# New due times and places for a few instructions in a fused attention and ELU-MLP kernel

## The chip, the cores and the metric

The kernel runs on one core of a Trainium2 chip. The metric is the device time of one execution in microseconds (us). The engines are TensorE (PE, matrix products; PEld its weight loads), VectorE (DVE), ScalarE (ACT), GpSimd (POOL) and SyncE (SP), whose queue issues nearly all DMAs. Each engine works through its own instructions in program order, and an instruction whose data isn't there holds up all behind it.

## The reference

```python
def _attn_ref(q, k, v, cap):            # 4 batches, 12 heads, 448 tokens, 64 wide
    scale = 1.0 / np.sqrt(q.shape[-1])
    scores = scale * np.matmul(q, k.transpose(0, 1, 3, 2))
    scores = cap * np.tanh(scores / cap)
    scores = scores - np.max(scores, axis=-1, keepdims=True)
    attn = np.exp(scores)
    attn = attn / (np.sum(attn, axis=-1, keepdims=True) + 1e-09)
    return np.matmul(attn, v).astype(np.float32)

def _moe_ref(x, w_in, w_out):           # 1792 tokens, 768 -> 2048 -> 768
    h = x @ w_in
    g = np.where(h > 0.0, h, np.exp(np.minimum(h, 0.0)) - 1.0)
    return (g @ w_out).astype(np.float32)
```

The heads of the attention's result, side by side, are the `x` of the second function. The inputs of the second function's weights are 64-bit numbers; the kernel makes 32-bit numbers of them on the chip.

## The kernel before

**Two parts.** The first, some 160 us, is the attention: 48 heads as 24 pairs, in 12 rounds of two pairs. The second is the MLP with its 2048 hidden features as 16 tiles, taken two at a time in 8 layers (r = 0 to 7). Its tokens lie in four blocks of 384, 384, 512 and 512; the first two are half 0 (h = 0), the other two half 1 (h = 1).

**Products.** 32-bit operands are held as a high part and a rest (`high`, `low`), and each product is three matmuls: high by high, rest by high, high by rest (L473, L474, L475). In the later layers, from layer 1 for half 1 and from layer 3 for half 0, the first product of the MLP is done by Strassen's scheme as seven products, numbered 1 to 7 (`block`; `m` in the trace). Some need *forms*: sums of token blocks, which are made once, written to memory (`send`, L351), and read in each layer (`fetch`, L361; `t<-form` in the trace) into a ring of three buffers and two more. A product has three parts in its contraction, so a fetch brings one third of what it needs. A number above 10 in the order means the product of half 0 (13 is product 3 of half 0), a triple such as (1, 1, 0) is the second product of the MLP for two output tiles, of the layer one back, block 1, tiles 0 and 1 (`pair`).

**Weights.** Each of 32 tiles is loaded by one DMA of 768 KB (`load`, L146) into one buffer, and made in steps (`steps`): two on ScalarE (L158, L161), three on VectorE (L169, L172, L185), one addition on GpSimd (L188), a high part and a rest. The step L185 is the last that reads the loaded data, so the next load waits for it.

**What sets the order in attention.** Every piece of work is entered as an event with a time written by hand (`AT`, `END`, `TANH`, `EXP`, in units of one of a round's seven score tiles), and the events, sorted by these times, are the program. The times set the order only. The parts that the change touches: `epsilon` (L1283 to L1288: VectorE, ScalarE, VectorE on one number in each row, which is added to the sums of exponentials), `take` (a numerator copied out of PSUM, L1063), `normalise` (L1092), `weights.run` (weight steps, two in each round that has some; in rounds 2, 5 and 9 it is one, which is L185 with GpSimd's L188), and at the end of attention `weights.run` twice, two steps on ScalarE and three that VectorE does. There `invert` (L1077) turns the sums of the round before the last into reciprocals; SP writes them to memory (L1079), reads them back over all rows (`spread`, L1087), and VectorE multiplies (`normalise`).

**What sets the order in the MLP.** `Plan.run` is a list scheduler. TensorE's order is fixed in the table `ORDERS`. All else is a step with an engine, an assumed duration, a due time, what it needs and gives, and which buffers it takes and frees; for each engine the step with the earliest due among those able to start is put next. Due times come from `DUES` (weights, per layer), `SMALL` (the forms of half 0, made in layers 1 to 3), `EARLY` and `REST` (what follows a product), and `LEAD` (fetches). Assumed times are not in the program: they only decide the order.

Of the kernel before, what the change touches and what calls it, by code (L numbers as in the profile page):

```python
# [53 lines left out]
    "add": ((2.55, 3.2), (6.05, 6.7)),  # L54
    "sums": 9.3, "take": (7.35, 7.95), "take_sums": 10.1,
    "invert": 15.3, "spread": (18.0, 18.01), "normalise": (21.4, 24.85),
    "prep": ((1.5, 1.85), (5.05, 5.4)), "load": (0.3, 5.5), "load_v": (0.2, 0.9),
    "weights": (4.8, 4.9), "wload": -0.5, "split": (-0.25, 1.3), "split_from": 5,
}
# [3 lines left out]

END = {"scored": -2.9, "unit0": 0.3, "weights": (0.5, 0.52)}

# [5 lines left out]
FROM = (3, 1)  # L71
LEAD = -5.1
DUES = (
    (-31.1, -11.1, -10.0, 1.1, 18.5),
    (-22.5, -19.0, -25.9, 2.0, 17.4),
    (-28.5, -23.8, -11.7, 6.1, 13.3),
    (-20.2, -13.3, -5.1, 7.4, 19.4),
)
# [14 lines left out]
    (  # L93
        1, 6, 2, (1, 3, 0), 7, (1, 3, 2), 11, 4, (1, 3, 4), 3, 5, (0, 2, 0), (0, 2, 2), 17, (0, 2, 4), 16,
        (0, 3, 0), (0, 3, 2), 14, 12, 13, 15, (0, 3, 4),
    ),
# [4 lines left out]
    (  # L101
# [3 lines left out]
    ),  # L105
)
SMALL = (-90.7, 23.7, 5.4)
EARLY, REST = (-3.8, -4.5, 4.5, -3.0, 9.6), (-1.1, 4.1, -5.8, -8.0, 2.7)
TAKES = {6: 2, 7: 3, 5: 1, 3: 4}
# [815 lines left out]
class Attention:  # L925
# [168 lines left out]
    def run(self, weights, moe, raw, rawv, scored):  # L1094
# [9 lines left out]
        end = NG * rounds  # L1104
# [5 lines left out]
        for n in range(rounds):  # L1110
# [7 lines left out]
            for i in range(2):  # L1118
# [9 lines left out]
                if p < NPAIR - NORMAL:  # L1128
                    at(min(g + AT["normalise"][i], end + 1.03), self.normalise, p)
                at(g + AT["load"][i], self.load, p + 4)  # L1130
# [8 lines left out]
            for k in range(2):  # L1139
                if k < WROUNDS.get(n, 0):  # L1140
                    at(g + AT["weights"][k], weights.run, 1)
                c = n - AT["split_from"]
                if 0 <= c < NC:
                    at(g + AT["split"][k], *((self.x.high, c, 0) if k == 0 else (self.x.low, c, 0)))
        for time, k in zip(END["weights"], (2, 3)):
            at(end + time, weights.run, k, True)
        for c in range(NC):
            at(end - 2 * NG + 1.5 * c + 1.0, self.x.park, c)
        at(1.5, epsilon, self.nc, self.con)
        at(end + END["scored"], scored)  # L1150
# [280 lines left out]
```

## Time and profile before

| | us |
|---|---|
| runs shown: median (lowest, highest) of 3 | 614.73 (613.46, 617.03) |
| profiled execution, its own time | 613.61 |
| its span, first to last instruction | 611.8 |
| TensorE busy | 597.8 (98%) |
| VectorE busy | 508.5 (83%) |
| ScalarE busy | 368.2 (60%) |
| GpSimd busy | 62.5 (10%) |
| TensorE's waits for fetched forms | 3.5, in two pieces |

The granted clock of TensorE was 0.997 of full over the span, so that no part of it is slowed. Times of the trace are counted from the span's start; the profiled execution's own time holds the span and 1.8 us around it. Where a row ends in square brackets, the engine was idle for so long before it, and what is named ended this.

### The profile page before, as it was taken

How to read it: one execution, taken by the hardware profiler on the slowest of the kernel's cores; microseconds unless marked ns; L12 is line 12 of the kernel's file. 1: busy time of each engine (PE TensorE's matmuls, PEld its weight loads, DVE VectorE, ACT ScalarE, POOL GpSimd, SP SyncE). 2: the span in 40 equal slices, each digit the busy share in tenths (PEclk: the TensorE clock that was granted, in tenths of full speed). 3: DMA queues.
4: the chain of work that ended last, by engine and by line, in shares of the span. 5: the costliest groups of instructions: out<-in, count | busy, mean ns of one | idle time of the engine just before them, and what ended most of it. 6: DMA issues, size and time to landing. Idle time of an engine off the chain costs nothing.

```text
span 611.8 us, 9149 instructions
## 1 busy us (share of the span) xinstructions
PE 597.8 (98%) x3302; PEld 465.4 (76%) x3302; DVE 508.5 (83%) x737; ACT 368.2 (60%) x550; POOL 62.5 (10%) x40
## 2 busy tenths in 40 slices
PE   8999999999999999999999999999999999989996
PEld 4444444444698889988988789898999889889985
DVE  4799999999879986998889888798786978887473
ACT  6999999999876774563564535546263444615130
POOL 0010010010101112111111211111112021111000
PEclk9999999999999999999999999999999999999998
DMA  6445645556421788878866788786678688756924
GB/s 219 147 126 182 219 126 180 176 179 230 150 73 51 293 277 298 304 243 301 295 234 256 284 292 286 276 278 255 241 248 270 250 284 279 243 181 224 307 112 187
DMA packets 61511, 138.49 MB, mean 226 GB/s; under 512 B 12562, under 2 KB 35090, under 8 KB 61458
## 3 DMA queue, kind: packets, MB, share of 16 engines
q1 hardware_dynamic: 61170, 137.30, 65.0%
q8 instruction: 28, 0.46, 0.3%
q10 hardware_dynamic: 288, 0.52, 0.3%
q14 instruction: 25, 0.20, 0.1%
HBM read 117.57 MB, written 20.14 MB: 225 GB/s over the span
## 4 chain that ended last, share of the span: by engine, by line
PE 89%; DMA 5%; DVE 3%; ACT 1%; SPq 1%; issue 1%; DVEq 0%
PE o L474 12%; PE o L475 12%; PE o L473 12%; PE m L473 8%; PE m L474 8%; PE m L475 8%; PE pv L1012 7%; PE s L968 6%; PE h L473 3%; PE h L474 3%; PE h L475 3%; PE sum L1056 3%; DMA t<-form 2%; DMA raw<-in_qk_dram 2%; PE pv L1025 1%; PE s L985 1%
## 5 line engine op out<-in xcount | busy, mean ns | idle before, releaser
L474 PE MATMUL o<-gl,wh 128*128 128x384 f32 (+1 forms) x380 | 137.7, 362 | 0.0
L473 PE MATMUL o<-gh,wh 128*128 128x384 f32 (+1 forms) x380 | 137.7, 362 | 0.0
L475 PE MATMUL o<-gh,wl 128*128 128x384 f32 (+1 forms) x380 | 137.7, 362 | 0.0
L544 DVE TENSOR_TENSOR x<-o,x 128x768 f32<-128x768 f32 (+1 forms) x83 | 89.5, 1085 | 26.5 <-PE o L475 26.4
L188 POOL TENSOR_TENSOR wv<-wv,wq 128x768 int32<-128x768 int32 x24 | 45.9, 1914 | 370.5 <-DVE wv L185 353.1
L1002 ACT ACTIVATE p<-s 128x896 f32<-128x896 f32 x84 | 72.4, 924 | 9.2 <-PE s L985 7.6
L473 PEld LDWEIGHTS o<-gh,wh 128*128 128x128 f32 x380 | 71.3, 188 | 8.1
L474 PEld LDWEIGHTS o<-gl,wh 128*128 128x128 f32 x380 | 71.3, 188 | 7.9
L475 PEld LDWEIGHTS o<-gh,wl 128*128 128x128 f32 x380 | 71.3, 188 | 7.6
L1006 ACT ACTIVATE p<-p 128x896 f32<-128x896 f32 x84 | 74.8, 955 | 0.0
L1012 PE MATMUL pv<-p,vf 128*64 128x448 f32 x276 | 57.2, 548 | 0.0
L158 ACT ACTIVATE wv<-pre 128x768 f32<-128x768 f32 x22 | 19.8, 899 | 47.3 <-DMA pre<-in_w_dram 47.3
L1012 PEld LDWEIGHTS pv<-p,vf 128*64 128x64 f32 x276 | 17.7, 136 | 37.7 <-issue 24.7
L517 ACT ACTIVATE gh<-e 128x384 fp32r<-128x384 f32 (+1 forms) x64 | 35.6, 570 | 16.5 <-DVE e L507 14.7
L521 DVE TENSOR_TENSOR gl<-e,gh 128x384 fp32r<-128x384 f32 (+1 forms) x64 | 40.7, 653 | 4.0 <-ACT gh L517 3.7
L195 ACT ACTIVATE wh<-wv 128x768 fp32r<-128x768 f32 x22 | 18.5, 841 | 42.4 <-POOL wv L188 42.1
L473 PE MATMUL m<-t,forms 128*128 128x512 f32 (+1 forms) x108 | 40.0, 371 | 1.0 <-DMA t<-form 1.0
L474 PE MATMUL m<-t,forms 128*128 128x512 f32 (+1 forms) x108 | 40.1, 371 | 0.0
L475 PE MATMUL m<-t,forms 128*128 128x512 f32 (+1 forms) x108 | 40.0, 370 | 0.0
L502 ACT ACTIVATE e<-c 128x512 f32<-128x512 f32 (+1 forms) x24 | 14.0, 584 | 42.1 <-DVE c L569 42.0
L503 ACT ACTIVATE e<-e 128x384 f32<-128x384 f32 (+1 forms) x64 | 37.1, 579 | 2.0
L569 DVE TENSOR_TENSOR u<-u,m 128x512 f32<-128x512 f32 (+1 forms) x48 | 29.2, 627 | 5.9 <-PE m L475 5.7
(148 smaller groups left out, 1174.3 us busy)
## 6 DMA issues: line engine op xcount, KB each, us to landing
t<-form SPq DMA_DIRECT2D x81, 512.0 KB, 5.4
pre<-in_w_dram SPq DMA_DIRECT2D x32, 768.0 KB, 5.8
t<-form SPq DMA_DIRECT2D x63, 384.0 KB, 5.6
raw<-in_qk_dram SPq DMA_DIRECT2D x22, 448.0 KB, 4.9
form<-t SPq DMA_DIRECT2D x12, 512.0 KB, 3.1
vf<-in_v_dram SPq DMA_DIRECT2D x23, 256.0 KB, 5.4
rb<-rec SPq DMA_DIRECT2D x48, 112.0 KB, 2.9
form<-stage SPq DMA_DIRECT2D x12, 384.0 KB, 4.0
```

Source lines behind the costliest of these rows:

```text
L188: nc.gpsimd.tensor_tensor(out=vi, in0=vi, in1=q, op=ALU.add)
L473: mm(acc, wh[:, m, :], ph, start=first, stop=False)
L474: mm(acc, wh[:, m, :], pl, start=False, stop=False)
L475: mm(acc, wl[:, m, :], ph, start=False, stop=last)
L503: self.nc.scalar.activation(out=e, in_=e, func=AF.Exp, scale=-1.0)
L517: self.nc.scalar.activation(out=self.g[k][0], in_=self.e[k], func=AF.Copy)
L521: self.nc.vector.tensor_tensor(out=gl, in0=self.e.pop(k), in1=gh.bitcast(F32), op=ALU.subtract)
L544: self.nc.vector.tensor_tensor(out=o, in0=self.o.pop((r, t, e)), in1=o, op=ALU.add)
L968: yield lambda a=a, b=b, i=i: self.nc.tensor.matmul(s, a[o, k], b[o, :S], start=i == 0, stop=i == 2)
L1002: self.nc.scalar.activation(out=pt, in_=self.s.pop((n, g)), func=AF.Tanh, scale=self.con.tanh_scale)
L1006: self.nc.scalar.activation(out=pt, in_=pt, func=AF.Exp, scale=self.con.exp_scale)
L1012: self.nc.tensor.matmul(out[o, :S], w[j], x[j], **flags)
```

## The change

It changes numbers in the tables and one line of the rule for rounds with a single weight step.

```diff
-    "sums": 9.3, "take": (7.35, 7.95), "take_sums": 10.1,
+    "sums": 9.3, "take": (6.72, 7.95), "take_sums": 10.1,
...
-    "weights": (4.8, 4.9), "wload": -0.5, "split": (-0.25, 1.3), "split_from": 5,
+    "weights": (4.8, 4.9), "added": 3.05, "wload": -0.5, "split": (-0.25, 1.3), "split_from": 5,
...
-END = {"scored": -2.9, "unit0": 0.3, "weights": (0.5, 0.52)}
+END = {"scored": -2.9, "unit0": 0.3, "weights": (-0.25, -0.24)}
...
-LEAD = -5.1
+LEAD = -4.4
 DUES = (
-    (-31.1, -11.1, -10.0, 1.1, 18.5),
+    (-27.0, -11.1, -20.8, 1.1, 18.5),
...
-        11, (1, 0, 0), 16, (1, 0, 2), 17, (1, 0, 4), 14, (1, 1, 0), 12, 13, (1, 1, 2), 15, (1, 1, 4), 1, 6,
+        11, (1, 0, 0), 16, (1, 0, 2), 17, (1, 0, 4), 13, 14, (1, 1, 0), 12, (1, 1, 2), 15, (1, 1, 4), 1, 6,
...
-SMALL = (-90.7, 23.7, 5.4)
-EARLY, REST = (-3.8, -4.5, 4.5, -3.0, 9.6), (-1.1, 4.1, -5.8, -8.0, 2.7)
+SMALL = (-78.4, 28.7, 5.4)
+EARLY, REST = (-3.8, -4.5, 4.5, -3.0, 12.8), (3.1, 2.6, -15.1, -8.0, 0.8)
...
-                    at(min(g + AT["normalise"][i], end + 1.03), self.normalise, p)
+                    at(min(g + AT["normalise"][i], end + 0.9), self.normalise, p)
...
-                    at(g + AT["weights"][k], weights.run, 1)
+                    alone = WROUNDS[n] == 1
+                    at(g + (AT["added"] if alone else AT["weights"][k]), weights.run, 1)
...
-        at(1.5, epsilon, self.nc, self.con)
+        at(4.6, epsilon, self.nc, self.con)
```

The other three rows of `DUES` change in the same way, and in layer 3 (the fourth table of `ORDERS`) products 11 and 12 each move ahead of one neighbour. From L1130 on every line of the changed file has a number higher by one.

**Attention.** Epsilon's step on ScalarE stood between the exponentials of score tiles 1 and 2 of the first round; it now stands behind that of tile 4. Its two steps on VectorE stood on both sides of L960 and L963 (the parts of a later query and key); they now stand behind the second addition of probabilities (L1046) of the first pair. In rounds 2, 5 and 9 L185, and GpSimd's L188 with it, stood ahead of L960 and L963; it now stands ahead of the copy of the sums (L1068) and of the second L1046 before them. The new times of `take` and `normalise` change no engine's order in rounds 0 to 10.

At the end of attention VectorE's order before was this (`den` the sums that are inverted, `num` a numerator, `wv` the weight tile in its making, `e` and `h` the first values of the MLP):

```order
L1077 RECIPROCAL den10_1801<-den10_1801 64x28
L1063 COPY num22_1867<-pv11_0_1789 128x448
L1092 TENSOR_TENSOR x_123<-num18_1593,rb18_1812 128x448
L169 TENSOR_SCALAR wv3_1872<-wv3_1872 128x768
L172 TENSOR_SCALAR wv3_1872<-wv3_1872 128x768
L185 SCALAR_TENSOR_TENSOR wv3_1872<-pre_73,wv3_1872 128x768
L1063 COPY num23_1880<-pv11_1_1835 128x448
L507 SCALAR_TENSOR_TENSOR e0_0_1908<-e0_0_1908,h0_1848 128x384
L1068 TENSOR_SCALAR sums11_1921<-sum11_1882,eps_88 128x448
```

and it is now:

```order
L1063 COPY num22_1843<-pv11_0_1789 128x448
L169 TENSOR_SCALAR wv3_1845<-wv3_1845 128x768
L172 TENSOR_SCALAR wv3_1845<-wv3_1845 128x768
L185 SCALAR_TENSOR_TENSOR wv3_1845<-pre_73,wv3_1845 128x768
L1077 RECIPROCAL den10_1801<-den10_1801 64x28
L1092 TENSOR_TENSOR x_123<-num18_1584,rb18_1812 128x448
L1063 COPY num23_1880<-pv11_1_1835 128x448
L507 SCALAR_TENSOR_TENSOR e0_0_1908<-e0_0_1908,h0_1858 128x384
L1068 TENSOR_SCALAR sums11_1921<-sum11_1882,eps_88 128x448
```

The inversion and the normalisation behind it now stand behind the copy of the numerator and behind all three weight steps. ScalarE's and SP's orders there are the same as before.

**The MLP, layers 2 and 3, SP's queue.** Rows with `t1_2_1_0<-form1_1_0` are the fetch of half 1, layer 2, form 1, first third; rows with `form0_...<-stage...` are sends of the smaller forms of half 0; `pre<-in_w_dram` is a weight load. Before:

```order
L351 DMA form0_2_2_3273<-stage2_2_3251 128x768
L146 DMA pre_73<-in_w_dram 128x1536
L361 DMA t1_2_1_0_3308<-form1_1_0_2279 128x1024
L361 DMA t1_2_1_1_3328<-form1_1_1_2326 128x1024
L351 DMA form0_4_2_3351<-stage4_2_3316 128x768
L361 DMA t1_2_1_2_3361<-form1_1_2_2379 128x1024
L361 DMA t1_3_2_0_3404<-form1_2_0_2473 128x1024
L146 DMA pre_73<-in_w_dram 128x1536
L361 DMA t1_3_2_1_3447<-form1_2_1_2500 128x1024
L361 DMA t1_3_2_2_3454<-form1_2_2_2545 128x1024
```

and now:

```order
L146 DMA pre_73<-in_w_dram 128x1536
L361 DMA t1_2_1_0_3296<-form1_1_0_2279 128x1024
L351 DMA form0_1_2_3312<-stage1_2_3286 128x768
L361 DMA t1_2_1_1_3334<-form1_1_1_2326 128x1024
L351 DMA form0_3_2_3345<-stage3_2_3310 128x768
L361 DMA t1_2_1_2_3356<-form1_1_2_2379 128x1024
L351 DMA form0_2_2_3380<-stage2_2_3354 128x768
L361 DMA t1_3_2_0_3393<-form1_2_0_2490 128x1024
L361 DMA t1_3_2_1_3415<-form1_2_1_2500 128x1024
L146 DMA pre_73<-in_w_dram 128x1536
L361 DMA t1_3_2_2_3444<-form1_2_2_2519 128x1024
L351 DMA form0_4_2_3467<-stage4_2_3441 128x768
```

Two sends now stand between the three fetches of form 1 where one stood, two more follow among the fetches of layer 3, and a weight load is ahead of the first fetch in both. Elsewhere six loads of weights change places with one neighbouring fetch each.

**The last layer, TensorE.** `m0_7` are the products of half 0 in layer 7, `t0_7_4_2` is the last third of form 4; the pair `o` stands ahead and behind. Before, product 4 came right behind the pair:

```order
L475 MATMUL o6_0_4_5560<-gh13_0_5444,wl27_5159 128x384
L473 MATMUL m4_0_7_5577<-t0_7_4_0_5539,wh29_5377 128x384
L474 MATMUL m4_0_7_5577<-t0_7_4_0_5539,wh29_5377 128x384
L475 MATMUL m4_0_7_5577<-t0_7_4_0_5539,wl29_5378 128x384
L473 MATMUL m4_0_7_5577<-t0_7_4_1_5543,wh29_5377 128x384
L474 MATMUL m4_0_7_5577<-t0_7_4_1_5543,wh29_5377 128x384
L475 MATMUL m4_0_7_5577<-t0_7_4_1_5543,wl29_5378 128x384
L473 MATMUL m4_0_7_5577<-t0_7_4_2_5553,wh29_5377 128x384
L474 MATMUL m4_0_7_5577<-t0_7_4_2_5553,wh29_5377 128x384
L475 MATMUL m4_0_7_5577<-t0_7_4_2_5553,wl29_5378 128x384
L473 MATMUL o6_1_0_5594<-gh12_1_5485,wh26_5056 128x384
```

and now product 3, on `forms` of the weights and resident tokens `x`, comes between (its last three matmuls are shown):

```order
L474 MATMUL m3_0_7_5580<-xl1_5_1829,forms_1895 128x384
L475 MATMUL m3_0_7_5580<-xh1_5_1828,forms_1895 128x384
L473 MATMUL m4_0_7_5594<-t0_7_4_0_5538,wh29_5377 128x384
L474 MATMUL m4_0_7_5594<-t0_7_4_0_5538,wh29_5377 128x384
L475 MATMUL m4_0_7_5594<-t0_7_4_0_5538,wl29_5378 128x384
L473 MATMUL m4_0_7_5594<-t0_7_4_1_5543,wh29_5377 128x384
L474 MATMUL m4_0_7_5594<-t0_7_4_1_5543,wh29_5377 128x384
L475 MATMUL m4_0_7_5594<-t0_7_4_1_5543,wl29_5378 128x384
L473 MATMUL m4_0_7_5594<-t0_7_4_2_5555,wh29_5377 128x384
L474 MATMUL m4_0_7_5594<-t0_7_4_2_5555,wh29_5377 128x384
L475 MATMUL m4_0_7_5594<-t0_7_4_2_5555,wl29_5378 128x384
L473 MATMUL o6_1_0_5609<-gh12_1_5486,wh26_5056 128x384
```

Nine matmuls of product 3 have moved from behind product 2 to ahead of product 4. SP's order of fetches in the last layer is the same.

## Rows read from the trace of the kernel before

**Rows 1.** The page, busy us of each engine, share of the span and instructions

```profile
PE 597.8 (98%) x3302; PEld 465.4 (76%) x3302; DVE 508.5 (83%) x737; ACT 368.2 (60%) x550; POOL 62.5 (10%) x40
```

**Rows 2.** Waits of TensorE: who waited for whom; us in all, times, longest

```profile
PE m L473 <- DMA t<-form: 3.5, 2, 2.5
...
PE sum L1056 <- DVE num L1063: 1.2, 2, 0.9
...
PE h L473 <- DVE e L507: 0.4, 1, 0.4
```

**Rows 3.** Timeline of ScalarE, first round: start, us, engine, line, operation [idle before]

```profile
12.21 0.20 ACT L1287 ACTIVATE eps<-eps 128x1 f32<-128x1 f32 x1 [0.50 <-DVE eps L1284]
12.32 1.77 ACT L1006 ACTIVATE p<-p 128x896 f32<-128x896 f32 x2
```

**Rows 4.** Timeline of TensorE, first round

```profile
18.21 0.47 PE L968 MATMUL s<-qkh 64*128 64x448 f32 x2 [0.71 <-ACT p L1002]
```

**Rows 5.** Timeline of VectorE, round 9, and the subtraction before it

```profile
118.40 1.03 DVE L963 TENSOR_TENSOR qkl<-raw,qkh 128x832 fp32r<-128x832 f32 x1
...
130.15 2.54 DVE L963 TENSOR_TENSOR qkl<-raw,qkh 128x832 fp32r<-128x832 f32 x1
```

**Rows 6.** Timeline of GpSimd, round 9

```profile
129.75 2.05 POOL L188 TENSOR_TENSOR wv<-wv,wq 128x768 int32<-128x768 int32 x1 [48.27 <-DVE wv L185]
```

**Rows 7.** Timeline of VectorE, end of attention

```profile
156.94 0.32 DVE L1077 RECIPROCAL den<-den 64x28 f32<-64x28 f32 x1 [0.25 <-DMA den<-sums]
157.18 0.55 DVE L1063 COPY num<-pv 128x448 f32<-128x448 f32 x1
...
158.87 0.55 DVE L169 TENSOR_SCALAR wv<-wv 128x768 f32<-128x768 f32 x1
...
160.93 0.62 DVE L1063 COPY num<-pv 128x448 f32<-128x448 f32 x1
...
167.20 0.31 DVE L1077 RECIPROCAL den<-den 64x28 f32<-64x28 f32 x1
...
177.34 0.62 DVE L1092 TENSOR_TENSOR x<-num,rb 128x448 f32<-128x448 f32 x1 [0.97 <-DMA rb<-rec]
...
178.96 1.89 DVE L285 TENSOR_TENSOR xl<-x,xh 128x512 fp32r<-128x512 f32 x3
```

**Rows 8.** Timeline of the SP queue, end of attention

```profile
159.80 1.09 SPq L1087 DMA_DIRECT2D rb<-rec  x2
```

**Rows 9.** Instructions of L146 near 161: duration min/median/max, starts; issue to landing

```profile
L146 SPq DMA_DIRECT2D pre<-in_w_dram x1: 433/433/433, 161.1 to 161.1; - x1
...
DMA to landing us min/median/max: 4.8/4.8/4.8
```

**Rows 10.** Instructions of L1071 near 163, the same view

```profile
L1071 SPq DMA_DIRECT2D den<-sums x4: 474/595/597, 162.6 to 164.4; - x4
...
DMA to landing us min/median/max: 2.2/2.6/3.4
```

**Rows 11.** Timeline of TensorE, second part, start

```profile
179.85 0.39 PE L473 MATMUL h<-xh,wh 128*128 128x512 f32 x1
```

**Rows 12.** The fetch (L361) issued at 304.8: us to landing

```profile
DMA to landing us min/median/max: 6.4/6.4/6.4
```

**Rows 13.** Timeline of TensorE, layer 2

```profile
311.88 0.39 PE L473 MATMUL m<-t,forms 128*128 128x512 f32 x1
```

**Rows 14.** Chain that ended last, layer 3: start, us, what

```profile
338.62 7.12 DMA t<-form
```

**Rows 15.** Timeline of TensorE, last layer

```profile
539.72 0.33 PE L473 MATMUL m<-t,forms 128*128 128x384 f32 x1
...
541.28 0.34 PE L473 MATMUL o<-gh,wh 128*128 128x384 f32 x1
...
550.81 0.44 PE L473 MATMUL m<-t,wh 128*128 128x384 f32 x1 [2.53 <-DMA t<-form]
```

**Rows 16.** Chain that ended last, last layer

```profile
544.08 6.69 DMA t<-form
```

More of the change, by code (lines that the diff above doesn't have):

```diff
@@ L71 @@
 FROM = (3, 1)
-LEAD = -5.1
+LEAD = -4.4
 DUES = (
-    (-31.1, -11.1, -10.0, 1.1, 18.5),
-    (-22.5, -19.0, -25.9, 2.0, 17.4),
-    (-28.5, -23.8, -11.7, 6.1, 13.3),
-    (-20.2, -13.3, -5.1, 7.4, 19.4),
+    (-27.0, -11.1, -20.8, 1.1, 18.5),
+    (-20.4, -19.0, -25.9, -8.4, 17.4),
+    (-26.8, -23.1, -11.7, 9.5, 13.3),
+    (-21.9, -13.3, -6.3, 7.4, 16.1),
 )
@@ L93 @@
     (
-        1, 6, 2, (1, 3, 0), 7, (1, 3, 2), 11, 4, (1, 3, 4), 3, 5, (0, 2, 0), (0, 2, 2), 17, (0, 2, 4), 16,
-        (0, 3, 0), (0, 3, 2), 14, 12, 13, 15, (0, 3, 4),
+        1, 6, 2, (1, 3, 0), 7, 11, (1, 3, 2), 4, (1, 3, 4), 3, 5, (0, 2, 0), (0, 2, 2), 17, (0, 2, 4), 16,
+        (0, 3, 0), 12, 14, (0, 3, 2), 13, 15, (0, 3, 4),
     ),
```

## The prediction

> **What bounds the kernel now.** I read the busy times first: TensorE is busy 597.8 of 611.8 us [rows 1], so the end is set by TensorE nearly everywhere, and a change that neither adds nor removes products can move the time only by what TensorE waits. The other engines' shares say little. The waits of TensorE came second: for forms fetched from memory 3.5 us in two pieces, for the copies of the attention numerators 1.2 us in two pieces [rows 2], and single waits below 1 us. The gap that starts the span and the tail behind TensorE's last product are not touched by the change. So I read, thirdly, the instructions around each wait and around each place where an instruction changes its place, on the engine that is waited for: is the late instruction late because of data, or because of its place in the queue?
>
> **The change part by part.**
>
> *Epsilon, at the start.* In the first round ScalarE waits 0.50 us until VectorE has made the first step of epsilon, which stands behind a cast that waits for its data; the pair of exponentials behind it starts at 12.32 [rows 3]. Without epsilon there it starts when ScalarE is free, 12.21 − 0.50 = 11.71, which is 0.61 earlier. Everything ScalarE does next is back to back, and TensorE waits for it once, 0.71 us before 18.21 [rows 4]. So 0.61 of these 0.71 go. Epsilon now stands behind a later exponential, when VectorE's step is long made, and costs ScalarE its own 0.20 [rows 3] at a point where TensorE no longer waits for it. Bounds: −0.71, the whole wait, and 0, if VectorE, which has the same instructions to do in each round, becomes late in ScalarE's place. I take −0.6, since a whole chain starts earlier by it.
>
> *GpSimd's step in rounds 2, 5 and 9.* The step of VectorE that releases GpSimd (L185) moves ahead by some instructions. A subtraction on VectorE (L963) takes 1.03 us alone and 2.54 us where it starts beside GpSimd's addition [rows 5], which runs from 129.75 for 2.05 us [rows 6]. So the collision costs 1.5 us of VectorE, and a later TensorE wait for VectorE's copies (1.2 us in two pieces [rows 2]) stands some microseconds behind two of the three places. After the change GpSimd's addition starts beside the second addition of probabilities (L1046), which reads two operands from on-chip memory as L963 does, and the copies that TensorE waits for stand behind both. So I take the 1.5 us to move from L963 to L1046: VectorE's sum up to the copies stays, and the term is 0. Bounds: −1.2, if L1046 runs free beside GpSimd and both waits go, and +0.9, if the third place gets a wait as long as the longer of the two [rows 2].
> The Trainium skill ("SBUF — State Buffer", section "Who interferes with whom") says that a VectorE instruction with two SBUF inputs and a GpSimd instruction that reads SBUF exclude each other, the first to start blocking the other. The trace agrees for L963 (2.54 against 1.03). By this rule the term is 0; were only L963 open to it, the term would be −1.2.
>
> *End of attention.* This is the part against the change. VectorE inverts the sums of the next-to-last round at 156.94, having waited 0.25 for them, then does a copy, a normalisation and the weight step of three instructions from 158.87 up to 160.93 [rows 7]. The new order puts the copy and these three ahead of the inversion. VectorE is free at 156.94 − 0.25 = 156.69; the copy takes 0.55 and the three 160.93 − 158.87 = 2.06, so the inversion starts at 159.3, 2.35 later. What hangs on it on SP goes in a fixed order: the reciprocals are spread at 159.80 [rows 8], then the load of the next weights at 161.1 [rows 9], then the four issues that collect the last sums, 162.6 to 164.4 [rows 10]. All of it moves by 2.35, except that the four were held only by the sums before: the load ends its issue at 161.1 + 0.43 + 2.35 = 163.9, so they start at about 163.9, 1.3 later. They then land at 164.4 + 1.3 + 2.2 = 167.9 by their own shortest latency [rows 10], or behind the weights, which land 4.8 us after 163.4 [rows 9], at 168.2, plus about 0.65 as before (164.4 + 2.2 = 166.6, against 161.1 + 4.8 = 165.9 for the weights): 168.9. The last inversion was at 167.20 [rows 7], so it is 0.7 to 1.7 late; I take 1.5, nearer to the second, which is what the trace shows of this pair of transfers. The chain goes on through memory without slack: the last normalisation, at 177.34, had waited 0.97 for it, and the subtractions behind it run to 178.96 and on [rows 7], three of them 1.89 us long. They feed TensorE's product at 179.85 [rows 11], whose operand, the first of the three, is done at about 178.96 + 1.89 / 3 = 179.6, some 0.2 earlier. So TensorE loses 1.5 − 0.2 = 1.3. Bounds: −0.4 (TensorE's one wait of 0.4 for the step of VectorE that now comes earlier goes [rows 2], and the collected sums are in time) to +1.9 (the whole shift, less the margins). The weight step that comes earlier earns nothing, since the weights it makes are used far later.
>
> *Layers 1 and 2 of the second part.* Fetches and sends move among each other on SP, for the smaller forms are due 12 us later. The place with least slack: a third fetch is issued at 304.8 and lands 6.4 later [rows 12], at 311.2, for a product at 311.88 [rows 13]: 0.6 to spare. Its issue stands behind a send that VectorE releases, before and after alike; one more 384 KB send now lies in its way on the channels. I take +0.2; bounds 0 (the margin holds) and +0.9.
>
> *Layer 3.* The fetch issued at 338.62 lands 7.12 later and stops TensorE for 1.0 us [rows 14]. SP's order around it, with a weight load ahead of it, is unchanged. I take 0, bounds −0.3 and +0.5.
>
> *Last layer.* TensorE waits 2.53 us before 550.81 [rows 15] for a fetch issued at 544.08 that takes 6.69 [rows 16]. That fetch is issued when the product ahead has given back a buffer, which stays as it is. The new order puts another product, nine matmuls on resident operands, ahead of the product that waits. Nine such take 541.28 − 539.72 = 1.56 us [rows 15]. The other two fetches of that product were in time already. So the wait shrinks by 1.56, and 1.0 to 1.1 of it stays: −1.55. Bounds: −2.53 (the fetch, having more time, is hidden fully) and −1.1, if it lands 0.43 later, by as much as the fetch of layer 3 took longer (7.12 [rows 14]).
>
> *Sum*: −0.6 + 0 + 1.3 + 0.2 + 0 − 1.55 = −0.65. The profiled execution took 613.61 (span 611.8), so its like would take 612.96. The median of the three other runs is 614.73; on it the same sum gives 614.1. I take the middle, 613.5, since one of the three lies far above the others.
>
> **The rivals.**
>
> *The end of attention costs nothing* (faster). For it: the four issues have 2.2 us at the least to land [rows 10], so that with little traffic they would be in time. Against it: the weights' load is in front of them, and the last normalisation waited 0.97 [rows 7], so nothing absorbs a shift. It gives −0.4 in place of +1.3: 613.5 − 1.7 = 611.8, and with the wait of layer 3 gone also, 610.8.
>
> *SP's queue stalls in layer 2* (slower than before). The sends wait for VectorE, and everything behind them on SP waits with them; more of them now stand ahead of fetches. From an issue later than 304.8 + 0.6 = 305.4 the product at 311.88 [rows 13] waits. If VectorE comes to such a send 3 us late, about three of its weight steps (each up to 0.96), TensorE waits 2.4, so the sum is −0.65 − 0.2 + 2.4 = +1.55: 615.7. For it: the 0.6 us are the smallest slack there. Against it: the instruction that releases the send stands where it stood.
>
> *The last layer doesn't gain* (the change doesn't do what it says). If the fetch is issued later by as much as the product moves, the wait stays, and the sum is +0.9: 615.05. Against it: the buffer is given back by a product that comes before both.
>
> **How the numbers follow.** Chances: my forecast 0.5, its own range 612.5 to 614.8 (the bounds at the end of attention and in the last layer partly against each other); no cost at the end of attention 0.2; SP's stall 0.12; no gain in the last layer 0.1; something else 0.08. The range 611.3 to 616.5 takes in the rivals, and leaves out their tails. What this kernel's measurement can tell from no change is about 0.5%, 3.1 us: below 611.66 the kernel is faster, above 617.80 slower. From the cases: faster 0.12 (half of the first rival, and a little of the rest), slower 0.06 (half of SP's stall, where a second fetch is late behind the first), the same 0.82.
>
> **What would show it.** Right: the wait of 0.71 in round 0 is down to 0.1; L963 is back at 1.03 and an L1046 takes 2.5; the inversion at 156.94 comes at 159, and a new wait of about a microsecond for VectorE stands near 180; the wait in the last layer is about 1.0. Wrong: no new wait near 180, a wait for a fetch between 305 and 325 above 1 us, or a wait in the last layer still above 2.

## The result, and the profile after

The changed kernel takes 617.31 us (median of 20 runs, 615.4 to 619.82), the kernel before 613.67 (20 runs, 611.88 to 617.03). The ratio is 1.0053, 95% interval 1.0037 to 1.0068: slower by about 3.3 us, where 0.65 less was forecast. Runs of one kernel spread by 4 to 5 us here, so a kernel's single profile can lie some us from its median: the profiled execution after took 618.83, the one before 613.61, 5.2 apart where the medians are 3.6 apart. Only what several profiles show is read as the change's.

TensorE's busy time, from the page of the changed kernel; it executes the same 3302 products, and they took 3.7 us longer [rows 1]:

```profile
PE 601.5 (97%) x3302; PEld 465.6 (75%) x3302; DVE 512.1 (83%) x737; ACT 369.5 (60%) x550; POOL 62.6 (10%) x40
```

TensorE's waits (us in all, times, longest):

```profile
PE m L473 <- DMA t<-form: 3.0, 7, 0.9
PE h L474 <- DVE xl L285: 1.8, 1, 1.8
...
PE sum L1056 <- DVE num L1063: 1.1, 3, 0.7
PE m L473 <- DVE c L569: 0.7, 1, 0.7
...
PE s L968 <- ACT p L1002: 0.4, 1, 0.4
```

The two waits for fetches, 3.5 in all [rows 2], have become seven smaller ones, 3.0 in all, and there is a new one of 1.8 for VectorE. The start went as forecast in kind. TensorE's row that answers to [rows 4] waits 0.44 instead of 0.71:

```profile
17.76 0.47 PE L968 MATMUL s<-qkh 64*128 64x448 f32 x2 [0.44 <-ACT p L1002]
```

In round 9 the stall moved from L963 to the addition L1046, as the prediction had it (VectorE's timeline, against [rows 5]):

```profile
127.63 2.42 DVE L1046 TENSOR_TENSOR u<-u,p 128x896 f32<-128x896 f32 x1
...
131.12 1.03 DVE L963 TENSOR_TENSOR qkl<-raw,qkh 128x832 fp32r<-128x832 f32 x1
```

The new wait is at the end of attention. VectorE's timeline there, which answers to [rows 7]:

```profile
156.26 0.62 DVE L1063 COPY num<-pv 128x448 f32<-128x448 f32 x1
156.79 0.55 DVE L169 TENSOR_SCALAR wv<-wv 128x768 f32<-128x768 f32 x1
...
157.97 0.96 DVE L185 SCALAR_TENSOR_TENSOR wv<-pre,wv 128x768 int32<-128x768 int32 x1
158.85 0.31 DVE L1077 RECIPROCAL den<-den 64x28 f32<-64x28 f32 x1
...
169.16 0.32 DVE L1077 RECIPROCAL den<-den 64x28 f32<-64x28 f32 x1 [2.21 <-DMA den<-sums]
...
179.29 0.63 DVE L1092 TENSOR_TENSOR x<-num,rb 128x448 f32<-128x448 f32 x1 [1.04 <-DMA rb<-rec]
179.83 0.69 DVE L285 TENSOR_TENSOR xl<-x,xh 128x512 fp32r<-128x512 f32 x1
...
180.90 1.89 DVE L285 TENSOR_TENSOR xl<-x,xh 128x512 fp32r<-128x512 f32 x3
```

The first inversion (L1077) starts at 158.85, 1.9 later than before, and the second, which had found its sums in place, now waits 2.21 for them and starts at 169.16, 1.96 later. The last normalisation is 1.95 later, and so are the subtractions (L285). SP's queue (the rows of [rows 8] and behind), and the four DMAs that collect the sums [rows 10]:

```profile
162.07 1.09 SPq L1087 DMA_DIRECT2D rb<-rec  x2
163.21 0.58 SPq L146 DMA_DIRECT2D pre<-in_w_dram  x1
163.83 2.39 SPq L1071 DMA_DIRECT2D den<-sums  x4
```

```profile
L1071 SPq DMA_DIRECT2D den<-sums x4: 474/596/597, 163.8 to 165.6; - x4
...
DMA to landing us min/median/max: 3.4/3.8/4.6
```

They are issued 1.2 later than before, and each takes 1.2 longer (3.4 to 4.6 against 2.2 to 3.4). What holds them is the weights' load: it lands at 165.87 in the kernel before and at 168.25 here, the first of the four at 166.05 in the one and 168.44 in the other, the last at 166.59 and 169.04. TensorE had come to this place 0.84 earlier than before (161.22 against 162.06) and waits all the longer:

```profile
178.40 0.40 PE L473 MATMUL h<-xh,wh 128*128 128x512 f32 x1
180.57 0.53 PE L474 MATMUL h<-xl,wh 128*128 128x512 f32 x1 [1.77 <-DVE xl L285]
...
181.33 0.63 PE L473 MATMUL h<-xh,wh 128*128 128x512 f32 x1
...
185.04 0.39 PE L474 MATMUL h<-xl,wh 128*128 128x512 f32 x1
```

The matmuls from 181.33 on take 0.63 where the same form takes 0.39 at 185.04. TensorE's granted clock by the microsecond (window, length, busy, matmuls, clock, DMA share, GB/s) shows why:

```profile
179.00:180.00 1.00, 0.00 (x0) 1.00 0.00 0
...
181.00:182.00 1.00, 1.00 (x4) 0.50 0.00 0
...
184.00:185.00 1.00, 1.00 (x5) 0.84 0.03 8
```

For 3.4 us it is 0.50, the lower of the two levels (1.2 of 2.4 GHz). The same products of the kernel before, and the subtraction whose result TensorE waits for in the changed kernel (it stands at 179.83 there):

```profile
177.89 0.69 DVE L285 TENSOR_TENSOR xl<-x,xh 128x512 fp32r<-128x512 f32 x1
```

```profile
179.16 0.39 PE L473 MATMUL h<-xh,wh 128*128 128x512 f32 x1
179.39 0.40 PE L474 MATMUL h<-xl,wh 128*128 128x512 f32 x1
...
182.12 0.39 PE L474 MATMUL h<-xl,wh 128*128 128x512 f32 x1
```

From the product at 178.40 to that at 185.04 the changed kernel takes 6.64, the kernel before 2.96 for the same ones (179.16 to 182.12). Of the 3.68 between them 1.94 lie ahead of the product at 180.57, and 1.74 behind it, where the clock is low (some 0.5 of these are lost there at a clock of 1.00 too, in the kernel with steps and copy below, where the next subtraction is late as well). They move TensorE from 0.76 ahead of the kernel before to 2.92 behind it.

Later, in the MLP, there are waits for fetches where the profile before had none (0.56 in layer 1, 0.87 in layer 7; the fetches from the chain that ended last), and the wait of the last layer [rows 15] is gone altogether:

```profile
239.34 7.80 DMA t<-form
```

```profile
574.17 6.96 DMA t<-form
```

### The profile page after: what moved, and what is told of

Read it like the earlier page. It is cut to its first block, busy times and chain, and to the rows that moved or that the text cites. A ratio compares the mean times of both kernels' runs of the same rounds, so it can differ in the third digit from the quotient of the medians.

```text
span 617.0 us, 9141 instructions
## 1 busy us (share of the span) xinstructions
PE 601.5 (97%) x3302; PEld 465.6 (75%) x3302; DVE 512.1 (83%) x737; ACT 369.5 (60%) x550; POOL 62.6 (10%) x40
## 4 chain that ended last, share of the span: by engine, by line
PE 79%; DMA 11%; DVE 6%; ACT 2%; issue 1%; SPq 1%; DVEq 0%; ACTq 0%
PE o L474 11%; PE o L473 11%; PE o L475 11%; PE m L473 8%; PE m L474 7%; PE m L475 7%; PE pv L1012 6%; PE s L968 5%; DMA t<-form 5%; PE h L474 2%; PE sum L1056 2%; PE h L475 2%; PE h L473 2%; DMA rb<-rec 2%; PE pv L1025 1%; DMA pre<-in_w_dram 1%
## 5 line engine op out<-in xcount | busy, mean ns | idle before, releaser
L544 DVE TENSOR_TENSOR x<-o,x 128x768 f32<-128x768 f32 (+1 forms) x83 | 89.3, 1084 | 23.5 <-PE o L475 23.4
L188 POOL TENSOR_TENSOR wv<-wv,wq 128x768 int32<-128x768 int32 x24 | 45.2, 1884 | 366.7 <-DVE wv L185 309.6
L521 DVE TENSOR_TENSOR gl<-e,gh 128x384 fp32r<-128x384 f32 (+1 forms) x64 | 44.0, 704 | 7.3 <-ACT gh L517 6.9
```

Source lines behind the costliest of these rows:

```text
L188: nc.gpsimd.tensor_tensor(out=vi, in0=vi, in1=q, op=ALU.add)
L521: self.nc.vector.tensor_tensor(out=gl, in0=self.e.pop(k), in1=gh.bitcast(F32), op=ALU.subtract)
L544: self.nc.vector.tensor_tensor(out=o, in0=self.o.pop((r, t, e)), in1=o, op=ALU.add)
```

## The experiments

Each kernel was timed beside the kernel before, in 11 or 12 runs (the two with `SMALL` split in 6). The ratio is to it, with its 95% interval.

| kernel | median, us | before, us | ratio | interval |
|---|---|---|---|---|
| weight steps at the end only | 615.27 | 613.9 | 1.0017 | 0.9991 to 1.0042 |
| attention's part without these | 612.75 | 613.9 | 0.998 | 0.9956 to 1.0004 |
| MLP's tables only | 614.96 | 613.9 | 1.0017 | 0.9995 to 1.004 |
| product 3 only | 613.72 | 613.9 | 0.9993 | 0.9971 to 1.0015 |
| changed, inversion first | 613.62 | 614.02 | 1.0001 | 0.9979 to 1.0022 |
| weight steps and copy | 615.95 | 614.02 | 1.0046 | 1.0022 to 1.007 |
| changed, weight steps put back | 614.99 | 614.02 | 1.0018 | 1.0 to 1.0036 |
| epsilon and product 3 | 611.96 | 614.02 | 0.997 | 0.995 to 0.999 |
| changed, load behind the sums | 617.07 | 613.96 | 1.0039 | 1.0014 to 1.0063 |
| changed, two steps ahead | 615.28 | 613.96 | 1.0012 | 0.9994 to 1.0031 |
| tables without product 3 | 615.39 | 613.96 | 1.0037 | 1.0015 to 1.0059 |
| epsilon, product 3, early steps | 613.63 | 613.96 | 0.9998 | 0.9976 to 1.0021 |
| tables, old times of smaller forms | 620.91 | 614.99 | 1.0103 | 1.0078 to 1.0127 |
| times of smaller forms only | 623.51 | 614.99 | 1.0135 | 1.0106 to 1.0163 |
| attention's part and product 3 | 612.7 | 614.99 | 0.9972 | 0.9952 to 0.9992 |

**The parts alone.** Four kernels, each the kernel before with one part of the change.

```diff
-END = {"scored": -2.9, "unit0": 0.3, "weights": (0.5, 0.52)}
+END = {"scored": -2.9, "unit0": 0.3, "weights": (-0.25, -0.24)}
```

> Before, with only the weight steps at the end of attention moved to -0.25. Theory (each part costs at its own place, and they add up): the three weight steps delay the inversion by about 1.9 us, the collected sums land behind the weight load, TensorE waits 1.5 to 2 us near 179, and its granted clock is half for some 3 us behind that wait, in most executions, which costs as much again: +2.5 to +3.5 us, 616.2 to 617.2 against 613.7. Rival (the waits for fetches in layers 1, 3 and 7 of the changed kernel come from this delay, since everything behind it meets other transfers): +4.5 or more. Rival (the clock is chance and not tied to the wait): +1.3.

The second kernel has the lines on `take`, `added`, `normalise` and `epsilon`:

> Before, with epsilon, GpSimd's step in rounds 2, 5 and 9, the copy of the numerator and the normalisation moved, and the weight steps at the end of attention as they were. Theory: -0.3 to -0.6 us from epsilon alone (the wait of 0.71 near 18 shrinks), nothing else, 613.2. Rival (TensorE's copies come late at another place): 0 or above.

The third has `LEAD`, `DUES`, `ORDERS`, `SMALL`, `EARLY` and `REST`:

> Before, with only the MLP's tables changed (due times, lead, orders of products, the smaller forms, what follows a product). Theory: the waits that the changed kernel shows for fetches near 242, 340, 350 and 576 and for VectorE near 445 come from these tables: about +1.3 + 1.7 + 0.8 + 0.8, less the 2.5 that the last layer gives back, so +1.5 to +2.5 us, 615.2 to 616.2. Rival (they come from the delay at the end of attention): -1.5 to -2.6, 611.1 to 612.2.

The fourth:

```diff
-        11, (1, 0, 0), 16, (1, 0, 2), 17, (1, 0, 4), 14, (1, 1, 0), 12, 13, (1, 1, 2), ...
+        11, (1, 0, 0), 16, (1, 0, 2), 17, (1, 0, 4), 13, 14, (1, 1, 0), 12, (1, 1, 2), ...
```

> Before, with only product 3 of half 0 ahead of product 4 in the last layer. Theory (the fetch is overlapped by all that stands ahead of it): the wait of 2.5 before 550.8 goes down to 1.0, -1.5 us, 612.2. Rival (the fetch also lands earlier, as in the changed kernel, where no wait was left): -2.5, 611.2. Rival (the fetch is issued later by as much): 0.

The weight steps alone gave +1.0, less than expected: without the earlier copy of the numerator VectorE's order is weight steps, inversion, copy, the inversion is 1.3 late (158.24), the last one 0.9 (168.12), and TensorE, itself later by a wait of 0.83 at 161, waits 0.18 near 180. Product against product (by the starts of the same ones in both profiles), TensorE loses 1.1 to the kernel before between 161 and 188, near the +1.0 of its time. Attention's other moves gave about −1.2, the interval reaching from −2.7 to +0.2. The tables gave +1.0, not the −1.5 to −2.6 of the rival: the MLP loses by itself. Product 3 alone gave −0.4, interval −1.8 to +0.9, which can't tell −1.5 from 0; the profiles can, below. The first three sum to +0.8, below the change's 3.3; the intervals, 2.8 to 3.1 wide each, nearly reach it, but the profiles show where the change loses more.

**The place of the inversion.** The changed kernel with the inversion ahead of the weight steps, and, separately, with the weight steps put back:

```diff
-                at(min(g + AT["invert"], end - 0.2), self.invert, n)
+                at(min(g + AT["invert"], end - 0.27), self.invert, n)
```

> The changed kernel, with the inversion of the sums put ahead of the three weight steps at the end of attention and all else as changed. Theory (the wait of TensorE near 179 and the low clock behind it come from the inversion's place alone): the inversion starts near 157, the last sums are inverted near 167, no wait above 0.3 near 179, no low clock there: -2.5 to -3.5 against the changed kernel's 617.3, 613.8 to 614.8. Rival (the tables of the MLP hold most of the loss): 616.5 to 617.3.

> The changed kernel, with the weight steps at the end of attention put back to where they were. Theory: as with the inversion first, without the wait near 179: 613.8 to 614.8. Rival (the tables of the MLP hold most of the loss): 616.5 to 617.3.

And the kernel before with the weight steps, the copy and the normalisation moved, so that VectorE's order at the end of attention is the changed one and all else as before:

> Before, with the weight steps at the end of attention moved and the copy of the numerator and the normalisation moved too, and nothing else; VectorE's order there is that of the changed kernel. Theory (the moved copy adds its 0.5 to the delay of the inversion, and TensorE, which no longer waits at 162, stands waiting for longer near 179): the last sums are inverted near 169.4, the wait near 179 is 1.5 to 2.0, and the clock is low for some 3 us behind it in most executions: +2 to +3.5, 616 to 617.4; more than with the weight steps alone (615.3, whose wait near 179 was 0.2). Rival (no difference to the weight steps alone): 615.3.

The first gives 613.62, all of the 3.3 us back by moving one instruction of 0.31 us (the ratios 1.0001 and 1.0053, whose intervals lie apart). In its timeline the inversions are at 157.05 and 167.69:

```profile
157.05 0.31 DVE L1077 RECIPROCAL den<-den 64x28 f32<-64x28 f32 x1
...
167.69 0.32 DVE L1077 RECIPROCAL den<-den 64x28 f32<-64x28 f32 x1 [0.47 <-DMA den<-sums]
...
177.82 0.63 DVE L1092 TENSOR_TENSOR x<-num,rb 128x448 f32<-128x448 f32 x1 [1.21 <-DMA rb<-rec]
```

In this profile the sums land as slowly as in the changed kernel (3.4 to 4.7 us), since the load takes 5.8; but they were issued 1.5 earlier, and the last inversion is only 0.5 later than before.

The second gives 614.99, just above its range. The third shows that these moves alone make a large part of the loss, +2.8 (interval +1.4 to +4.3). Its TensorE waits as the changed kernel's does:

```profile
181.50 0.50 PE L474 MATMUL h<-xl,wh 128*128 128x512 f32 x1 [1.59 <-DVE xl L285]
```

The profiles say that the copy moved ahead was the missing part (the times alone don't, as the intervals of the first kernel and of this one overlap): it adds its 0.5 to the delay, and it also takes away TensorE's wait at 161, by which TensorE arrives earlier at the chain that is late. In this execution the clock stayed at 1.00 behind the wait, unlike in the changed kernel's profile.

**How much delay.** The changed kernel with the third weight step behind the inversion:

```diff
-        for time, k in zip(END["weights"], (2, 3)):
+        for time, k in zip((-0.25, -0.24, -0.1), (2, 2, 1)):
```

> The changed kernel, with two of the three weight steps ahead of the inversion and the third behind it, so that the inversion is some 0.9 us less late. Theory (the wait grows with the inversion's delay once the slack of about 0.3 is used): the last sums are inverted near 168.3, the wait near 179 is 0.7 to 1.1 instead of 1.8: -0.8 to -1.5 against the changed kernel, 615.8 to 616.5. Rival (a step: the third weight step releases the load, and the load alone decides): no change, 617.3. Rival (any delay below 1 is absorbed): 613.8 to 614.5.

The second inversion is at 167.83, and TensorE waits 0.89, between 0.1 and 1.77; the time is 615.28, between the two as well, though 0.5 below the range given:

```profile
179.12 0.50 PE L474 MATMUL h<-xl,wh 128*128 128x512 f32 x1 [0.89 <-DVE xl L285]
```

**Where the sums wait.** The changed kernel with the load of the next weights behind the four issues that collect the sums, on SP alone:

```diff
-            Step("d", 2.4, due - 11.0, wt.load, needs=(("raw", k - 1),)),
+            Step("d", 2.4, due - 11.0, wt.load, needs=(("raw", k - 1), *(("taken",) if k == 4 else ()))),
...
-            Step("v", 0.7, -9.0, self.take_sums, n, needs=("summed",), frees=(("sums",),), psum=True),
+            Step("v", 0.7, -9.0, self.take_sums, n, needs=("summed",), frees=(("sums",),), psum=True, gives="taken"),
```

> The changed kernel, with one difference on one queue: on SP the load of the next weights at the end of attention comes behind the four issues that collect the last sums, not ahead of them. The inversion stays as late as in the changed kernel. Theory (the sums are late because SP issues them late and because they land behind the weights): the four are issued near 163.2 instead of 163.8 and land in 2.2 to 2.7 us instead of 3.4 to 4.6, the last inversion is near 167.4 instead of 169.2, the wait near 179 is gone: -2.5 to -3.2, 614.1 to 614.8. Rival (it is the late inversion itself, through its spread, and not the sums): no change, 617.3.

This failed as a cure, and the rival had the time right: 617.07. The sums now land in 1.9 to 2.3 us and the last inversion is at 166.76, earlier than in the kernel before. But the reciprocals that it writes stand behind the load now, and behind two sends, which land 5.7 and 7.2 us after their issue (2.5 and 2.9 in the kernel before). SP's queue, and the time to landing of the write (L1080, issued at 167.10):

```profile
162.68 2.52 SPq L1072 DMA_DIRECT2D den<-sums  x4
165.30 0.52 SPq L146 DMA_DIRECT2D pre<-in_w_dram  x1
...
167.10 0.63 SPq L1080 DMA_DIRECT2D rec<-den  x1
...
168.89 8.06 SPq L1088 DMA_DIRECT2D rb<-rec  x6
```

```profile
DMA to landing us min/median/max: 6.7/6.7/6.7
```

6.7 us for a transfer that takes 2.6 in both other traces (issued 167.54, landed 170.12 before; 169.51 and 172.07 after), so that the normalisation that ends a wait at 173.08 in the kernel before does so at 175.05, and TensorE waits 1.62. Both orders come to the same: one of the chain's small transfers stands behind 768 KB, and the delay of the load by the late inversion sets when these have passed. In all 16 profiles with the load ahead, the first of the four DMAs that collect the sums lands 0.17 to 0.21 after the load, whether it was issued 0.63 or 1.54 behind it, and whether the load took 4.5 or 5.8. The Trainium skill ("DMA: Bandwidth & Descriptors", section "Queues, rings and completion order") says that on each DMA engine the descriptors of one queue are taken in the order of the ring; both traces agree.

**The last layer and the tables.** What TensorE waits at each place of the MLP, summed from the gaps between its matmuls in each profile (us; epsilon and product 3 is the kernel of that name in the table, and so on):

| profile | layer 1 | layer 2 | layer 3 | VectorE, 440 to 535 | last layer | fetch behind it |
|---|---|---|---|---|---|---|
| before | 0 | 0 | 1.02 | 0 | 2.53 | 0 |
| weight steps only | 0.32 | 0 | 0.53 | 0 | 0.79 | 0.72 |
| attention's part | 0 | 0 | 1.89 | 0 | 0.28 | 0 |
| weight steps and copy | 0.32 | 0 | 1.63 | 0 | 0.54 | 0.38 |
| product 3 only | 0.76 | 0 | 2.11 | 0 | 0 | 0.88 |
| epsilon and product 3 | 0 | 0 | 0.51 | 0 | 0 | 0.78 |
| these and early steps | 0.05 | 0 | 0.73 | 0 | 0.37 | 0.18 |
| attention's part and product 3 | 0 | 0 | 2.24 | 0 | 0 | 0.76 |
| changed | 0.56 | 0 | 1.72 | 0.67 | 0 | 0.87 |
| tables only | 0.54 | 0 | 0.90 | 0 | 0 | 0.57 |
| changed, inversion first | 0.57 | 0.49 | 1.70 | 0.49 | 0 | 0.46 |
| changed, two steps ahead | 0 | 0.81 | 2.18 | 0.46 | 0 | 0.48 |
| changed, weight steps back | 0.21 | 1.03 | 1.98 | 0 | 0 | 0 |
| changed, load later | 0.55 | 0.41 | 2.00 | 0 | 0 | 0.98 |
| tables without product 3 | 0.95 | 0.81 | 1.49 | 0.13 | 0.07 | 0 |

The first eight have the old tables, four of them with product 3 moved. With the old tables the waits in layers 1 to 3 sum to 1.5 in the mean, with the new ones to 2.7, and 0.25 for VectorE comes on top. Where product 3 has its old place among the old tables, the last layer's wait is 2.53, 0.79, 0.28 and 0.54; with product 3 ahead, product 4 waits in none of ten profiles (the 0.37 is for another product). In the second of the four the fetch took 4.88 us (chain that ended last), against 6.69 in [rows 16]:

```profile
545.23 4.88 DMA t<-form
```

Two things have to be known of such sums. They hold idle time alone, and a wait costs more: one product begins 0.23 after another and takes 0.39, and a wait loses this overlap too. TensorE's time from the product at 187.73 of the kernel before to the last one, less its idle time and what a low clock costs, is 414.9 in the profile with two waits and 417.1 in that with twelve. And the profiled executions of the seven kernels with the new tables took 1.2 longer than their kernels' medians in the mean, those of the eight with the old ones 0.1. The two work against each other, so the price of the tables is better read from the times: +1.0 alone, with an interval from −0.3 to +2.5.

The wait of layer 2 is the place of the rival on SP's queue. In the kernel with the weight steps back, SP issues three fetches of form 1 with sends between them, and the last at 309.27, where the kernel before, whose products ran 2.2 us earlier there, had it at 304.8:

```profile
303.06 0.32 SPq L361 DMA_DIRECT2D t<-form  x1
306.92 0.32 SPq L351 DMA_DIRECT2D form<-stage  x1
307.33 0.38 SPq L361 DMA_DIRECT2D t<-form  x1
308.85 0.32 SPq L351 DMA_DIRECT2D form<-stage  x1
309.27 0.37 SPq L361 DMA_DIRECT2D t<-form  x1
```

Each send waits for VectorE's half of the form (L345), and the fetch waits behind it. The rival's mechanism is there in five of seven profiles, with 0.4 to 1.0 instead of the 2.4 that it was priced at.

The tables without the new place of product 3 were run to see what it is worth among them:

> Before, with the MLP's tables changed except the place of product 3 in the last layer. Theory (the tables lose in layers 1 to 3 and product 3's place wins about 1 us in the mean, since the wait it shortens was 0.3 to 2.5 in the traces with the old order): 1 us more than with all tables, 615.0 to 616.2, and a wait of 0.3 to 2.5 near 550. Rival (product 3's place wins nothing in the mean): as with all tables, 614.9.

615.39, a ratio of 1.0037 against 1.0017 with it; the intervals overlap. The profile shows no wait in the last layer there (0.07), so this does not decide what product 3 brings among the new tables.

Two kernels were to tell the smaller forms' times from the rest: all tables with the old `SMALL`, and the new `SMALL` alone.

> Before, with all tables of the MLP changed except the due times of the smaller forms. On SP one send instead of two stands between the three fetches of form 1 in layer 2. Theory (the later sends of the smaller forms hold SP up in layer 2 and load the channels in layers 2 and 3): the wait near 313 is gone, the waits from 336 to 363 are 1.0 to 1.3 in all instead of 1.7, and the time is 0.5 to 1.5 below that with all tables (615.0), 613.5 to 614.5. Rival (the weights' due times do it): no change, 615.0, waits as with all tables.

> Before, with only the due times of the smaller forms changed. Theory: waits near 313 and from 336 to 363 grow, by 0.5 to 1.5 in all, 614.5 to 615.5, with the wait near 550 as in the old order (0.3 to 2.5). Rival (the tables hurt only together): 613.9.

Both missed on the other side: 620.91 and 623.51. With the new `SMALL` alone, TensorE waits 5.1 us for VectorE's additions of outputs (L544), 3.5 of it before 324, and its clock is low behind that wait (with the old `SMALL` and all other tables it is one wait of 4.4 at the same place):

```profile
PE o L473 <- DVE x L544: 5.1, 2, 3.5
PE m L473 <- DMA t<-form: 4.4, 9, 1.0
```

```profile
322.00:324.00 2.00, 0.00 (x0) 0.86 0.08 31
...
326.00:328.00 2.00, 2.00 (x6) 0.50 0.00 0
...
330.00:332.00 2.00, 2.00 (x10) 0.94 0.25 104
```

VectorE's order there has the sums and rests of the weight forms (L241, L251) ahead of the addition that gives PSUM back. So the times of one table fit the others: changed singly, they give an order that loses at a place where neither kernel waits. Which number of the tables makes the waits of layers 1 to 3 stays open.

**What won, together.** Epsilon and product 3, these with the early weight steps behind the inversion, and the whole of attention's part (weight steps aside) with product 3:

> Before, with only epsilon moved and product 3 ahead of product 4 in the last layer. Theory (these two parts are the gains of the change): -0.5 from epsilon and -0.3 to -2.5 from the last layer, since the wait there differs between executions: -0.8 to -2.0, 611.9 to 613.1 against 613.9. Rival (epsilon's gain is lost again at the end of attention, where the chain of the sums sets the time): -0.3 to -1.5.

> Before, with epsilon moved, product 3 ahead of product 4 in the last layer, and at the end of attention the copy of the numerator, the inversion and then the three weight steps in this order (early weight steps that no longer delay the inversion). Theory: 612.0, as with epsilon and product 3 alone, or up to 0.4 below by the wait that goes near 162, which is then waited near 179. Rival (the early weight load still hurts the sums): 613 to 614.

> Before, with all of the attention's part except the weight steps at the end, and product 3 ahead of product 4 in the last layer: a version that takes what has won. Theory: -1 to -2.5, 611.5 to 613. Rival (moving GpSimd's step in three rounds costs what epsilon wins): 613.5 or above.

The first gives 611.96, ratio 0.997, interval 0.995 to 0.999: faster than the kernel before by 1.8 us, and, as the intervals of the two ratios lie apart, faster than the changed one too. The third gives the same, 0.9972. The second, 613.63, is where its rival had it, though its interval overlaps with that of the first. In its profile the inversions are as early as before (157.14 and 167.18), yet the last normalisation is 0.7 later (178.04) and TensorE loses 0.5 between 161 and 188. No gain by early weight steps shows. TensorE's waits for fetches in the first, one in layer 3 and one in the last layer:

```profile
PE m L473 <- DMA t<-form: 1.1, 2, 0.8
```

## Why the prediction was wrong

The signs that the prediction named came nearly all as it said: the wait in round 0 shrank, the stall went to an L1046, the inversion came at 159, and a new wait for VectorE stood near 180. They tested the places. What failed were the sizes of the terms.

*Epsilon* (−0.6): right in kind. TensorE's wait near 17 is 0.71 to 0.76 in the eight profiles without the move and 0 to 0.44 in eight of the nine with it; in the ninth, attention's part with product 3, it is 0.85 all the same. The mean of the nine is 0.24 where 0.1 was forecast, so the wait shrinks by about 0.5. The prediction has TensorE wait once for this chain, but six of the eight profiles without the move have another wait ahead of it, at 13 to 14, for the exponentials behind epsilon (0.23 in the kernel before, 1.42 at the most), and none of the nine with it. Other delays take up part of both: at 35 us TensorE is 0.3 earlier with the move in the mean, where single profiles differ by over 1.

*GpSimd's step* (0): right, the stall of VectorE moved from L963 to L1046 (2.42 against 1.08 to 1.09 alone). TensorE's waits for the copies of numerators sum to 1.4 in the mean of the profiles with the move and of those without.

*The end of attention* (+1.3, bounds −0.4 to +1.9): the mechanism was right at each link, from the inversion's delay to the subtractions near 180, and the term was too small: 3.3 us come back when the inversion alone is put in front (613.62 against 617.31), and +2.8 appear when only these moves are made. Four steps of it failed. First, the margin of 0.2 was read from the wrong product: the one at 179.85 [rows 11] reads high parts (`xh`), not what the subtractions make. The one that waits in the changed kernel had 0.8 to spare (179.39, after a subtraction that ends at 178.58), so this error was against the change. Second, TensorE's own gains ahead of this place (0.4 of the wait at 161) were entered as a lower bound, that is as a gain, while in front of a chain that doesn't wait for TensorE they only lengthen the wait. Third, the last sums were inverted 0.4 later than I took (169.16, and 167.20 + 1.5 = 168.7), at the later of my two estimates. These three bring the term to about its upper bound: product against product, TensorE loses 1.8 between 161 and 188 with steps and copy and 2.1 with the load behind the sums, both at a clock of 1.00. Fourth, the clock was not in the sum at all; with it the changed kernel's profile loses 3.3 there. It falls in some executions only. A mean granted clock of 0.996 or less was recorded in 12 of 42 executions of the three kernels with a wait of 1.6 to 1.8 near 180 (6 of 20 of the changed one), in 9 of 120 of the kernel before in the experiments, and in 12 of 132 of the eleven other kernels with 12 executions each. In the changed kernel these 6 executions average 618.9 us and the other 14 616.7, so that the clock makes some 0.6 of its 617.3, and most of the loss is there without it. The estimate by these numbers, 1.8 to 2.1 and 0.6, gives 2.4 to 2.7 of the 2.8 to 3.3; the rest lies within the intervals.

*Layers 1 and 2* (+0.2) and *layer 3* (0): wrong. TensorE's waits in layers 1 to 3 rise by 1.2 in the mean of the profiles, and those for VectorE add 0.25. The step that failed was to price one profile's waits as if they were fixed. With one and the same order, layer 3's wait was between 0.5 and 2.2. The rival on SP's queue was half right: its place and its mechanism, not its price.

*Last layer* (−1.55): the wait went fully, where 1.0 to 1.1 was to stay. But it had been 2.53 only in the execution that was profiled; the four profiles with the old order average 1.0, so about 1.0 is won, and 0.3 of it given back at the next fetch (0.28 in the mean of these four, 0.60 in the ten with product 3 ahead). The step that failed was taking a fetch's 6.69 us as its time; it took 4.88 in the other trace.

So the forecast's sum −0.65 came out at about +3.3 by +1.1 to +2 at the end of attention, and by some 2 us in the tables, whose gain of 1.55 was 0.7 and whose cost of 0.2 was about 1.45. That these two give +0.75 for the tables, near the +1.0 of their times, is as far as they are confirmed.

## What to carry to other kernels

An instruction of 0.3 us that feeds a chain of transfers is worth more than the 2 us of work put ahead of it: where SP's queue carries small transfers of a chain and a large load that a weight step releases, move neither without following the chain to the engine that waits for it. A gain ahead of such a chain is waiting time at its end, and an estimate of a wait on TensorE needs a second line for the clock behind it. A wait for a transfer read from one profile is a draw, not a size; read it from several executions of the same order before pricing a change by it.

## What was not expected of the hardware

The granted clock of TensorE fell to 0.50 behind waits of 1.77 (changed kernel), 2.11 (product 3 only, layer 3), 3.5 and 4.4 us (the two kernels with `SMALL` split), for 3.4 to 6.8 us. It stayed at 1.00 behind waits of 2.53 (before, last layer), 1.59 (steps and copy) and 1.62 us (load behind the sums). So the length of the wait alone does not tell; what does is left open here.

A mean of the granted clock over the span can mislead. In the profile before it is 0.997, and all that it lacks comes from the last microseconds, behind TensorE's last product, where the clock is 0.50 (0.53 in the window from 608 to 610). It doesn't say that no product was slowed: the first score products (L968) take 0.57 up to 10.06 us and 0.36 from 10.79 on.
